# A planner's model of transfers gets figures of its own for the start of the program, and nineteen ranks of a fused attention and MoE kernel are moved

## The chip, the cores and the metric

The kernel runs on one core of a Trainium2 chip. The engines are PE (matrix products; PEld is its loading of weights), DVE and ACT (elementwise work), POOL and SP (here they issue transfers). The metric is the device time of one execution in microseconds, lower is better.

## The reference

Eight batches of eight heads, 512 local and 32 global tokens a batch, head size 64. A local query sees the 32 global keys and the local keys within 32 places; a global query sees all 544 keys. The outputs of all heads of a token, put side by side (512 wide), go through a layer with a hard swish.

```python
s_g = scale * np.matmul(q_g, k_all.transpose(0, 1, 3, 2))
out_g = np.matmul(sm(s_g), v_all)
s_ll = scale * np.matmul(q_l, k_l.transpose(0, 1, 3, 2))
mask = np.abs(pos[:, None] - pos[None, :]) <= window
s_ll = np.where(mask, s_ll, -1000000000.0)
s_lg = scale * np.matmul(q_l, k_g.transpose(0, 1, 3, 2))
a_l = sm(np.concatenate([s_lg, s_ll], axis=-1))
out_l = np.matmul(a_l, np.concatenate([v_g, v_l], axis=2))
...
h = x @ w_in                       # (4352, 512) @ (512, 2048)
g = h * np.clip(h + 3.0, 0.0, 6.0) / 6.0
out = g @ w_out                    # (4352, 2048) @ (2048, 512)
```

## The kernel before

**Planned, not looped.** The body does not emit instructions in the order of its loops. `add` records an operation with its engine (or a choice of two), its planned duration, what it depends on, the buffer rings it takes and frees, and a `key`, its rank. `Plan.lay` then plays these operations on a model of the engines: at each moment it starts, on each engine, the operation that can start soonest, and among those that can start within 40 ns of it the one with the lowest key. A copy that ACT or DVE may do goes to the one that would finish it first. The order found in this way is emitted, and each engine runs its own queue in that order. So a key or a planned time does nothing to the chip but through the order of the queues, the choice of ACT or DVE, and `Plan.fill`, which puts idle matmuls ("filler", line 1017) on PE where the plan sees it wait before the first use of the second A bank: a filler step is planned at 440 ns (twice that before 5 us) and their number is the planned gap divided by that.

**Transfers.** The model of transfers (`Transfers`) has two queues, POOL's loads and SP's, which share the DMA engines. A transfer of so many packets of so many ns each begins `FIRST` after its issue and takes packets x ns / 16, slower when both queues are busy (`BESIDE`, `EVEN`). A queue has eight lanes: a transfer is issued when the eighth before it has landed. A row load has 12.4 ns a packet, a w_in or w_out load 85, a strip 86 or 300.

**The stages of a batch b.** `load_qk` (line 410) brings q and k of 128 tokens (one j of four), `load_v` V in five pieces (i of five), `load_g` the global q and k of two batches. The transfers from POOL are issued in the order of their keys alone. `turn_qk` and `turn_g` transpose by PE, through PSUM ring T (one buffer) or M (three), and a copy; from batch 4 or 5 on SP transposes by DMA. `strips_moved` lays V out as overlapping strips `st`, by seven transfers that SP issues once V is in (batch 0: some by copies, `strips_kept`). `place_kg` puts the global keys in place. `local_step` (b, j) is one attention step of 128 queries: scores on PE into the one S buffer (lines 655 to 669), eight masked reductions on DVE (681), eight exponentials on ACT (692), normalising on DVE (702, 706), eight transposes on PE (713), a copy, products with the strips on PE into the banks A0 and A1 (735, 743; two half steps from batch 1 on), and copies into `xt`. `global_steps` does the global queries (781 to 856); it takes S, A0 and A1. `moe_local` then makes the first product of a batch, w_in times `xt` (`first`, line 870), its hard swish on ACT (877) and DVE (881), and the second, with w_out (`second`, line 894), and SP stores the result (908).

**Ranks.** Steps of batch b get keys near 4b, and loads lie earlier by `AHEAD`. For batch 0 the list `seq` ranks the loads one by one (from -8.0 in steps of 0.05: q0 to q3, v0 to v4, w_in, then the global loads); w_out follows from -6.0 on, among batch 1's loads (from -6.6 in steps of 0.1).

```python
self.queue[o.eng].append([o.start + self.FIRST[o.eng] + wait, packets * ns / 16, o])
...
s, o = min(((s, o) for s, o in starts if s <= s0 + 40), key=lambda x: (x[1].key, x[1].n))
...
n = round(gap / one) if at < self.EARLY else int((gap - 100) / one)
```

Of the kernel before, what the change touches and what calls it, by code (L numbers as in the profile page):

```python
# [75 lines left out]


class Plan:  # L80
# [4 lines left out]
    COLD, FILL, EARLY = 5000.0, 440.0, 12000.0  # L85
# [123 lines left out]
def kernel(  # L209
# [20 lines left out]
    NJ = Sl // P  # L230
# [712 lines left out]

    xgd = {}
    lqk, lg, keyT, kg0_op = {}, {}, {}, []
    for b in range(B):
        if b == 0:
            seq, APART = ["q0", "h", "q1", "q2", "v0", "v1", "v2", "q3", "v3", "v4", "i0", "i1", "i2", "i3", "g"], (0.11, 0.001)  # L950
            for n, what in enumerate(seq):
                k, i, key = what[0], int(what[1:] or 0), -8.0 + 0.05 * n
                if k == "q":
                    lqk[0, i] = load_qk_direct(0, i, key) if i < 2 else load_qk(0, i, key, 1, APART[i - 2])
                elif k == "h":
                    halo = load_halo(key)
                elif k == "g":
                    lg[0] = []
                    for n, (i, k) in enumerate(((0, 0), (0, 1), (1, 0), (1, 1))):
                        lg[0].append(load_g(0, i, k, key + 0.001 * n, lg[0][0] if n else None))  # L960
                elif k == "v":
                    vload[0, i] = load_v(0, i, key)
                else:
                    wi[i] = load_w_in(i, key)
            for c in range(0, NDFF, 4):
                wo[c] = wo[c + 1] = wo[c + 2] = wo[c + 3] = load_w_out(c // 4, W_OUT + 0.05 * c)
        else:
            base = -6.6 if b == 1 else 4.0 * b - 3.0 - AHEAD
            stepk = 0.1 if b == 1 else 0.4
            for j in range(NJ):  # L970
                lqk[b, j] = load_qk(b, j, base + j * stepk)
            if b % 2 == 0:
                lg[b // 2] = []
                for i in range(2):
                    for k in range(2):
                        lg[b // 2].append(load_g(b, i, k, base + (1.5 + 0.1 * i + 0.05 * k) * stepk,
                                                 lg[b // 2][0] if lg[b // 2] else None))
            for i in range(NV):
                vload[b, i] = load_v(b, i, base + (i + 3.5) * stepk)
        if b == 0:  # L980
            for js in BLOCKS:
                s_ = (strips_kept if js[0] < KEEP else strips_moved)(b, list(js), 4.0 * b - 3.5 + 0.9 * js[0])
                for j in js:
                    strip[b, j] = s_
        else:
            for j in range(NJ):
                strip[b, j] = strip[b, j - 1] if j else strips_moved(b, list(range(NJ)), base + 1)
        strip[b] = {j: strip[b, j] for j in range(NJ)}
        lead = 4.0 * b - 4.0 if b < 2 else 4.0 * b - AHEAD
        if b % 2 == 0:  # L990
            if b == 0:
                head = turn_direct(0, lqk[0, 0], halo)
                kg[0] = head.pop()
                gT[0] = turn_g(0, lg[0], lead + 0.5, [kg[0]])
                if KEEP < NJ:
                    kg0_op.append(place_kg(0, lead - 1.2 if KEEP == 0 else lead + 0.9, kg[0]))
            else:
                gT[b // 2] = turn_g(b, lg[b // 2], lead - 1.5)
        if b:
            kg[b] = place_kg(b, lead - 1.2)  # L1000
        for j in range(NJ):
            if b == 0 and j < 2:
                o = turn_direct(j, lqk[0, j]) if j else head
                qkT[0, j], keyT[0, j] = o[0], o[1:]
            elif b == 0:
                keyT[b, j] = [turn_qk(b, j, lqk[b, j][:1], lead + j - 1.5, (1,))]
                qkT[b, j] = turn_qk(b, j, lqk[b, j], lead + j - 1.5, (0,))
            else:
                qkT[b, j] = turn_qk(b, j, lqk[b, j], lead + j - 1.5)
# [3 lines left out]
        xgd[b] = global_steps(b, lead + 3.6)  # L1013
        moe_local(b, 4.0 * b + 0.5, 4.0)
    moe_global(4.0 * b + 2.5, 1.5)

    order = plan.fill(plan.lay(), lambda: nc.tensor.matmul(  # L1017
        out=psA[1][:, 0:256], lhsT=idle.bitcast(FP32)[:, 0:P], rhs=idle.bitcast(FP32)), "A1")
# [36 lines left out]
```

## Time and profile before

| what | us |
|---|---|
| median of 3 runs (lowest to highest) | 333.57 (333.43 to 334.77) |
| the profiled execution's own time | 332.85 |
| its span, first to last instruction | 331.1 |
| PE busy | 317.9 (96%) |
| DVE busy | 265.3 (80%) |
| ACT busy | 254.0 (77%) |
| POOL busy | 106.1 (32%) |
| transfers of the POOL queue, share of 16 engines' span | 71.3% |
| transfers of the SP queue, the same | 46.5% |

How to read it: times are microseconds from the first instruction. A line of the profile names source line, engine, operation and the tiles it writes and reads; `x8` is a count. "idle before" and `<-` tell how long an engine stood idle before an instruction and what released it. PE's busy time counts a matmul from its start to a modelled end, so waits can hide in it; starts are exact. A row of the stage table gives a stretch, its length, then busy time and instruction count of PE, PEld, DVE, ACT and POOL, the granted PE clock as a share of full speed, the DMA share and GB/s.

### The profile page before, as it was taken

The numbers are of one execution on the slowest core, as the hardware profiler recorded it, in microseconds if no ns is written. First come the engines' busy times: TensorE is split into PE (matmuls) and PEld (weight loads), VectorE is DVE, ScalarE is ACT, GpSimd is POOL, SyncE is SP. The second block draws the span as 40 slices with busy tenths as digits, with TensorE's granted clock in tenths as the row PEclk, the third lists the DMA queues.
The fourth block names the chain that finished last, engine by engine and source line by source line (L and its number), as shares of the span: only waits on it lengthen the run. The fifth ranks groups of instructions, "written<-read, shape, count | busy, mean of one in ns | idle before, by whom it ended". The sixth has DMA issues, their size and how long they took to land.

```text
span 331.1 us, 10240 instructions
## 1 busy us (share of the span) xinstructions
PE 317.9 (96%) x3824; PEld 184.9 (56%) x3824; DVE 265.3 (80%) x997; ACT 254.0 (77%) x851; POOL 106.1 (32%) x139
## 2 busy tenths in 40 slices
PE   8999968989999999999999999999999999999996
PEld 6778855456556554555554545454445544546644
DVE  4899799779998799898998799689988896385400
ACT  4899798579989499887995789699988994464402
POOL 8725942497292845613460050004000000000000
PEclk9999999999999999999999999999999999999999
DMA  9999999999999999999999999999984214400013
GB/s 160 184 251 172 128 196 264 161 200 223 218 174 206 203 157 174 214 225 168 129 176 250 242 122 194 197 193 178 205 135 120 63 36 110 91 0 2 32 56 104
DMA packets 158738, 52.25 MB, mean 158 GB/s; under 512 B 142944, under 2 KB 151392, under 8 KB 158688
## 3 DMA queue, kind: packets, MB, share of 16 engines
q0 software_dynamic: 106560, 17.05, 71.3%
q1 hardware_dynamic: 52128, 34.55, 46.5%
q8 instruction: 30, 0.49, 0.6%
q14 instruction: 20, 0.16, 0.2%
HBM read 35.26 MB, written 8.91 MB: 133 GB/s over the span
## 4 chain that ended last, share of the span: by engine, by line
PE 64%; DVE 15%; ACT 9%; issue 2%; ACTq 0%; DVEq 0%
PE m L894 31%; PE m L870 24%; DVE gs L881 4%; ACT sm L692 3%; DVE sm L681 3%; PE a L743 3%; ACT t L877 2%; DVE pn L706 2%; PE s L669 2%; DVE pg L821 2%; ACT sg L807 2%; PE t L713 1%; PE s L662 1%; ACT xt L296 1%; DVE et L298 1%
## 5 line engine op out<-in xcount | busy, mean ns | idle before, releaser
L894 PE MATMUL m<-wout,gs 128*128 128x512 f16 (+1 forms) x560 | 129.7, 373 | 0.0
L870 PE MATMUL m<-xt,win 128*128 128x512 f16 (+1 forms) x576 | 122.1, 355 | 1.8 <-DVE gs L881 0.9
L692 ACT ACTIVATE sm<-sm,stat 128x128 f32<-128x128 f32 x256 | 100.9, 398 | 11.1 <-DVE stat L681 10.5
L881 DVE SCALAR_TENSOR_TENSOR gs<-t,m 128x512 f16<-128x512 f32 x136 | 91.6, 683 | 17.2 <-ACT t L877 15.9
L877 ACT ACTIVATE t<-m 128x512 f32<-128x512 f32 x136 | 80.7, 599 | 22.2 <-PE m L870 21.1
L870 PEld LDWEIGHTS <-win 128*128 128x128 f16 x640 | 59.3, 98 | 52.5 <-issue 3.3
L894 PEld LDWEIGHTS <-gs 128*128 128x128 f16 x560 | 51.1, 98 | 49.9 <-issue 1.4
L681 DVE CUSTOM_DVE_ANT_0 sm<-s,mask 128x128 f32<-128x128 f32 x256 | 61.7, 282 | 2.2 <-PE s L669 1.1
L692 ACT ACTIVATION_READ_ACCUMULATOR sm<-sm,stat 128x1 f32 x256 | 50.0, 195 | 0.0
L706 DVE TENSOR_TENSOR pn<-sm,stat 128x512 f16<-128x512 f32 x64 | 44.0, 687 | 0.6
L296 ACT CAST xt<-a 64x256 f16<-64x256 f32 (+1 forms) x83 | 31.0, 374 | 7.5 <-PE a L743 6.6
L411 POOL DMA_DIRECT2D ve<-in_v_l_dram x40 | 32.2, 822 | 10.6 <-PE t L592 6.5
L411 POOL DMA_DIRECT2D nat<-in_q_l_dram x30 | 27.0, 900 | 25.4 <-DMA qk<-nat 10.7
L411 POOL DMA_DIRECT2D nat<-in_k_l_dram x30 | 27.4, 915 | 15.6 <-DMA win<-in_moe_w_in_dram 5.2
L743 PEld LDWEIGHTS <-st 128*128 128x128 f16 x448 | 19.7, 98 | 11.3 <-issue 1.0
L296 ACT COPY ot<-m 128x512 f32<-128x512 f32 (+1 forms) x24 | 13.6, 571 | 13.2 <-PE m L894 12.7
L411 POOL DMA_DIRECT2D ve<-in_v_g_dram x8 | 4.8, 597 | 56.3 <-PE a L848 56.2
L743 PE MATMUL a<-et,st 128*128 128x64 f16 x448 | 22.1, 193 | 0.6 <-ACT xt L296 0.6
L681 DVE DVE_READ_ACCUMULATOR2_ANT stat<- 128x1 f32 x256 | 21.1, 82 | 0.0
L298 DVE CAST xt<-a 64x256 f16<-64x256 f32 (+1 forms) x33 | 14.1, 428 | 4.4 <-PE a L743 4.1
L702 DVE RECIPROCAL stat<-stat 128x4 f32<-128x4 f32 x64 | 11.1, 173 | 5.9 <-ACT sm L692 5.3
L1017 PE MATMUL a<-idle 128*128 128x256 f32 x46 | 14.6, 450 | 1.2 <-DVE idle L380 1.2
(88 smaller groups left out, 270.7 us busy)
## 6 DMA issues: line engine op xcount, KB each, us to landing
out_dram<-ot SPq DMA_DIRECT2D x31, 256.0 KB, 3.5
st<-ve SPq DMA_DIRECT2D x14, 384.0 KB, 7.4
nat<-in_k_l_dram POOLq DMA_DIRECT2D x30, 128.0 KB, 8.0
nat<-in_q_l_dram POOLq DMA_DIRECT2D x30, 128.0 KB, 8.4
st<-ve SPq DMA_DIRECT2D x7, 512.0 KB, 7.5
st<-ve SPq DMA_DIRECT2D x14, 256.0 KB, 7.7
ve<-in_v_l_dram POOLq DMA_DIRECT2D x24, 128.0 KB, 6.7
st<-ve SPq DMA_DIRECT2D x18, 128.0 KB, 7.3
```

The source lines that it names most:

```text
L296: nc.scalar.copy(out=out, in_=in_)
L298: nc.vector.tensor_copy(out=out, in_=in_)
L411: nc.gpsimd.dma_start(out=dst(op), in_=src)
L681: nc.vector.tensor_tensor_reduce(out=sm[sm_op.slot][:, h, :], in0=psS[s.slot][:, e, p * P:(p + 1) * P], in1=m, scale=-scale, scalar=3.0e38 ...
L692: nc.scalar.activation(out=sm[sm_op.slot][:, h, :], in_=sm[sm_op.slot][:, h, :], func=EXP, scale=-1.0, bias=stat[stat_op.slot][:, 0, h:h + 1],
L706: (nc.gpsimd if op.eng == "POOL" else nc.vector).tensor_tensor(out=pn[pn_op.slot][:, h0:h1, :], in0=sm[sm_op.slot][:, h0:h1, :], in1=stat[ ...
L743: nc.tensor.matmul(out=psA[a][:, c0:c0 + 64], lhsT=st[r][:, u * NJ + j, p * P:(p + 1) * P], rhs=et[et_op.slot][:, 2 * p:2 * p + 2, u * UQ: ...
L870: nc.tensor.matmul(out=psM[op.slot][:, i * n:(i + 1) * n], lhsT=w_in_t[:, m, (c + i) * P:(c + i + 1) * P], rhs=x()[:, m, t0:t0 + n], start ...
L877: nc.scalar.activation(out=t1[to.slot], in_=psM[f.slot], func=RELU, bias=0.5, scale=1.0 / 6.0)
L881: nc.vector.scalar_tensor_tensor(out=gs[set_.slot][:, c:c + k, t0:t0 + n], in0=t1[to.slot].rearrange("f (k t) -> f k t", k=k), scalar=1.0, ...
L894: nc.tensor.matmul(out=psM[(f or op).slot][:, 0:w], lhsT=gs[set_.slot][:, c, t0:t0 + P], rhs=w_out_t[:, c, cols], start=(c == 0), stop=(c ...
L1017: order = plan.fill(plan.lay(), lambda: nc.tensor.matmul(out=psA[1][:, 0:256], lhsT=idle.bitcast(FP32)[:, 0:P], rhs=idle.bitcast(FP32)), "A1")
```

## The change

`Transfers` gets other figures for what is issued early. Until 28 us (`EARLY`, which was 12 us and stood for something else) a row load counts 14.0 ns a packet in place of 12.4, a weight load 70.5 in place of 85, a short strip 75 in place of 86, and the two queues share by packet size alone. Until 13 us (`FULL`) a transfer begins later than `FIRST` says: from SP by 670 ns before 6 us and 3130 after, from POOL by 700 before 4 us and 470 after; before, SP's began 1000 later until 12 us.

`MOVED` adds an amount to nineteen ranks. A negative one makes the operation come earlier in its queues, as far as the plan lets it; an entry with two parts moves every load of its kind.

```diff
-    LANES, END, EARLY, LATE = 8, 300, 12000.0, 1000.0
+    LANES, END, EARLY, FULL = 8, 300, 28000.0, 13000.0
+    OF_EARLY = {12.4: 14.0, 85.0: 70.5, 86.0: 75.0}
...
-        wait = self.LATE if o.eng == "SP" and o.start < self.EARLY else 0
+        wait = 0
+        if o.start < self.EARLY:
+            ns = self.OF_EARLY.get(ns, ns)
+        if o.start < self.FULL:
+            wait = (670 if o.start < 6000 else 3130) if o.eng == "SP" else 700 if o.start < 4000 else 470
...
-            part = {h[2].eng: h[2].dma[1] + self.EVEN for h in heads}
+            even = 0 if self.now < self.EARLY else self.EVEN
+            part = {h[2].eng: h[2].dma[1] + even for h in heads}
...
+    MOVED = {("step", 0, 0): -1, ("step", 0, 3): -0.25, ("turn", 0, 2): 1, ("v", 0, 4): -1, ("w_in", 0): 0.5,
+             ("q", 1, 3): -0.5, ("step", 1, 1): 1, ("step", 1, 3): -2, ("v", 1, 2): 0.5, ("v", 1, 4): -1,
+             ("g", 2): -0.25, ("v", 2, 1): -0.5, ("v", 2, 3): -4, ("g", 4): 2, ("step", 4, 0): -0.5,
+             ("step", 5, 0): -0.5, ("step", 6, 2): 0.25, ("step", 6, 3): 0.25, ("step", 7, 3): 0.5}
...
+        def by(what, j=None):
+            return MOVED.get((what, b), 0.0) + MOVED.get((what, b, j), 0.0)
...
-            xdone[b, j] = local_step(b, j, lead + j)
+            xdone[b, j] = local_step(b, j, lead + j + by("step", j))
```

The other lines of the diff add `by(...)` in the same way to the keys of the loads (`q`, `g`, `v`, `w_in`, `w_out`), the strips, `turn_g`, the placing of keys, `turn_qk`, the global steps and the products; only the nineteen entries above are not zero. `Plan.EARLY`, a constant of `fill`, stays at 12 us.

In the queues as built, POOL's first load is now v(0,4); the four global loads of batches 0 and 1 stand ahead of the four of w_in; among the loads of batch 1, j = 3 of q and k and the last piece of V come before the others, and the piece v(1,2) stands behind three of the four w_out loads; v(2,3) comes right after the first q and k of batch 2. On PE the first scores of batch 0 come before the turn of its third q and k, the globals of batch 0 are turned right after the third scores (they were turned after nine groups of first products), batch 0's global step comes after four of its sixteen groups of first products (it came after eight), batch 1's steps run in the order 0, 1, 3, 2, and batch 0's second products all come before batch 1's products with the strips.

More of the change, by code (lines that the diff above doesn't have):

```diff
@@ L953 @@
                 if k == "q":
-                    lqk[0, i] = load_qk_direct(0, i, key) if i < 2 else load_qk(0, i, key, 1, APART[i - 2])
+                    lqk[0, i] = load_qk_direct(0, i, key) if i < 2 else load_qk(0, i, key + by("q", i), 1, APART[i - 2])
                 elif k == "h":
@@ L961 @@
                 elif k == "v":
-                    vload[0, i] = load_v(0, i, key)
+                    vload[0, i] = load_v(0, i, key + by("v", i))
                 else:
-                    wi[i] = load_w_in(i, key)
+                    wi[i] = load_w_in(i, key + by("w_in", i))
             for c in range(0, NDFF, 4):
-                wo[c] = wo[c + 1] = wo[c + 2] = wo[c + 3] = load_w_out(c // 4, W_OUT + 0.05 * c)
+                wo[c] = wo[c + 1] = wo[c + 2] = wo[c + 3] = load_w_out(c // 4, W_OUT + 0.05 * c + by("w_out", c // 4))
         else:
@@ L975 @@
                     for k in range(2):
-                        lg[b // 2].append(load_g(b, i, k, base + (1.5 + 0.1 * i + 0.05 * k) * stepk,
+                        lg[b // 2].append(load_g(b, i, k, base + (1.5 + 0.1 * i + 0.05 * k) * stepk + by("g"),
                                                  lg[b // 2][0] if lg[b // 2] else None))
             for i in range(NV):
-                vload[b, i] = load_v(b, i, base + (i + 3.5) * stepk)
+                vload[b, i] = load_v(b, i, base + (i + 3.5) * stepk + by("v", i))
         if b == 0:
             for js in BLOCKS:
-                s_ = (strips_kept if js[0] < KEEP else strips_moved)(b, list(js), 4.0 * b - 3.5 + 0.9 * js[0])
+                s_ = (strips_kept if js[0] < KEEP else strips_moved)(b, list(js), 4.0 * b - 3.5 + 0.9 * js[0] + by("strips", js[0]))
                 for j in js:
@@ L986 @@
             for j in range(NJ):
-                strip[b, j] = strip[b, j - 1] if j else strips_moved(b, list(range(NJ)), base + 1)
+                strip[b, j] = strip[b, j - 1] if j else strips_moved(b, list(range(NJ)), base + 1 + by("strips"))
         strip[b] = {j: strip[b, j] for j in range(NJ)}
@@ L997 @@
             else:
-                gT[b // 2] = turn_g(b, lg[b // 2], lead - 1.5)
+                gT[b // 2] = turn_g(b, lg[b // 2], lead - 1.5 + by("turn_g"))
         if b:
-            kg[b] = place_kg(b, lead - 1.2)
+            kg[b] = place_kg(b, lead - 1.2 + by("keys"))
         for j in range(NJ):
@@ L1005 @@
             elif b == 0:
-                keyT[b, j] = [turn_qk(b, j, lqk[b, j][:1], lead + j - 1.5, (1,))]
-                qkT[b, j] = turn_qk(b, j, lqk[b, j], lead + j - 1.5, (0,))
+                keyT[b, j] = [turn_qk(b, j, lqk[b, j][:1], lead + j - 1.5 + by("turn", j), (1,))]
+                qkT[b, j] = turn_qk(b, j, lqk[b, j], lead + j - 1.5 + by("turn", j), (0,))
             else:
-                qkT[b, j] = turn_qk(b, j, lqk[b, j], lead + j - 1.5)
+                qkT[b, j] = turn_qk(b, j, lqk[b, j], lead + j - 1.5 + by("turn", j))
                 keyT[b, j] = [qkT[b, j]]
         for j in range(NJ):
-            xdone[b, j] = local_step(b, j, lead + j)
-        xgd[b] = global_steps(b, lead + 3.6)
-        moe_local(b, 4.0 * b + 0.5, 4.0)
-    moe_global(4.0 * b + 2.5, 1.5)
+            xdone[b, j] = local_step(b, j, lead + j + by("step", j))
+        xgd[b] = global_steps(b, lead + 3.6 + by("global"))
+        moe_local(b, 4.0 * b + 0.5 + by("products"), 4.0 + by("span"))
+    moe_global(4.0 * b + 2.5 + by("products_g"), 1.5)
     order = plan.fill(plan.lay(), lambda: nc.tensor.matmul(
```

4 lines of the change are left out of this document (2 added, 2 removed).

## The prediction

> **What bounds the kernel now.** I read the page first, then the busy time by stage.
>
> ```profile
> span 331.1 us, 10240 instructions
> ...
> 8.70:24.90 16.20, 14.93 (x373) 11.90 (x373) 14.57 (x75) 14.56 (x58) 8.12 (x12) 1.00 1.61 219
> 24.90:34.00 9.10, 8.93 (x128) 7.90 (x113) 8.22 (x29) 8.40 (x27) 5.23 (x6) 1.00 1.69 163
> 34.00:42.90 8.90, 8.43 (x166) 7.30 (x165) 7.21 (x17) 7.10 (x17) 8.90 (x13) 1.00 1.90 138
> 42.90:50.80 7.90, 4.60 (x99) 3.86 (x97) 7.82 (x43) 7.20 (x28) 3.56 (x5) 1.00 1.35 204
> 50.80:60.80 10.00, 10.00 (x140) 5.64 (x139) 9.81 (x46) 8.42 (x40) 1.28 (x3) 1.00 1.25 260
> 60.80:74.10 13.30, 11.42 (x142) 6.92 (x142) 9.51 (x23) 8.52 (x29) 11.32 (x15) 1.00 1.90 171
> ...
> 80.00:240.00 160.00, 158.43 (x1929) 85.30 (x1928) 145.95 (x558) 136.82 (x477) 55.86 (x70) 1.00 1.48 192
> 240.00:320.00 80.00, 80.00 (x684) 41.92 (x682) 52.53 (x155) 50.93 (x151) 0.00 (x0) 1.00 0.30 65
> ```
>
> Each stage row gives its length, then the busy time of PE, PEld, DVE, ACT and POOL, the clock, the DMA share. From 80 to 320 us PE is busy 238.43 of 240 us: 1.57 us in all can be won there. Up to 24.9 us PE's busy time is partly its idle-filling matmuls; DVE (14.57 of 16.20) and ACT (14.56) carry the softmax of batch 0. Between 24.9 and 74.1 PE idles 5.8 us (0.17, 0.47, 3.30, 0, 1.88). So a new order can win time before 74 us, and little after.
>
> PE in order of time, where it loses most:
>
> ```profile
> 42.93 0.44 PE L835 MATMUL t<-ident,pg 128*128 128x128 f16 x5
> 44.99 0.44 PE L835 MATMUL t<-ident,pg 128*128 128x128 f16 x5 [1.62 <-ACT eg L296]
> 45.37 0.35 PE L662 MATMUL s<-kgz,qk 128*128 128x32 f16 x8
> ...
> 48.29 0.39 PE L713 MATMUL t<-ident,pn 128*128 128x128 f16 x4
> ...
> 50.75 0.35 PE L662 MATMUL s<-kgz,qk 128*128 128x32 f16 x8 [0.87 <-DVE stat L681]
> ...
> 67.09 1.03 PE L894 MATMUL m<-wout,gs 128*128 128x512 f16 x4
> 68.58 0.39 PE L743 MATMUL a<-et,st 128*128 128x64 f16 x8 [0.46 <-ACT xt L296]
> 69.77 0.38 PE L612 MATMUL t<-ident,natg 128*128 128x128 f16 x4 [0.80 <-DVE et L298]
> ...
> 74.09 0.35 PE L662 MATMUL s<-kgz,qk 128*128 128x32 f16 x8
> ```
>
> From start to start, less about what the step itself takes: 42.93 to 44.99 loses 1.7 (five transposes take 0.38, 44.99 to 45.37), 48.29 to 50.75 loses 2.0, 67.09 to 68.58 loses 0.6, 68.58 to 69.77 loses 0.95. That is 5.25; with the smaller gaps I put it at 7. In the first two, PE stands behind a one-buffer ring (T, S).
>
> **The change, part by part.** The transfer figures emit no instruction; they shift planned starts, and with the 19 ranks they re-sort the queues. The built orders hold the same steps (438 on PE, 134 on POOL, 143 on SP), one filler step less on PE, and 60 copies that change between ACT and DVE. The first 82 PE steps, up to batch 2's first scores (74.09 above), are one set in both. So the sum is: when PE comes to that step, and what is lost behind it.
>
> *The first 28 us.*
>
> ```profile
> 3.48 2.34 PE L1017 MATMUL a<-idle 128*128 128x256 f32 x5
> 5.62 1.24 PE L459 MATMUL m<-ident,sm 128*128 128x128 f32 x8
> ...
> 7.22 0.46 PE L459 MATMUL m<-ident,t 64*128 64x64 f32 x4
> ...
> 8.70 0.24 PE L655 MATMUL s<-qk 64*32 64x96 f16 x8
> ...
> 24.90 1.92 PE L870 MATMUL m<-xt,win 128*128 128x256 f16 x16
> ...
> 13.26 0.74 POOL L411 DMA_DIRECT2D win<-in_moe_w_in_dram  x1
> ...
> win<-in_moe_w_in_dram POOLq DMA_DIRECT2D x1, 512.0 KB, 17.0
> ...
> 17.70 0.58 POOL L411 DMA_DIRECT2D natg<-in_k_g_dram  x1
> ...
> natg<-in_k_g_dram POOLq DMA_DIRECT2D x1, 32.0 KB, 13.4
> ...
> sm<-in_k_l_dram SPq DMA_DIRECT2D x1, 256.0 KB, 6.2
> ...
> 24.10 0.56 ACT L296 CAST xt<-a 128x512 f16<-128x512 f32 x1
> ...
> 35.49 0.39 DVE L628 COPY kgz<-gt 64x128 f16<-64x128 f16 x2
> 36.02 0.69 DVE L298 COPY qk<-t 128x1024 f16<-128x1024 f16 x1
> 36.63 1.22 DVE L794 TENSOR_REDUCE stat<-s 128x2 f32<-128x1024 f32 x1
> ...
> 38.34 0.68 DVE L881 SCALAR_TENSOR_TENSOR gs<-t,m 128x512 f16<-128x512 f32 x1
> ```
>
> Four filler steps stand at the start, not five: the first turn comes at 4.8, not 5.62 (a filler step is two matmuls of 0.43 to 0.47, from the first row). Two fillers now stand before the halo turn: 6.8, not 7.22. The turn of keys 2 (turn(0,2) +1, step(0,0) -1) no longer stands before the first scores: about 8.05, not 8.70. That 0.65 isn't kept. The second k load (issued near 3.9, in 6.2 later, at 10.1) holds the next step. The key copy of batch 1, 0.5 on DVE (35.49 to 36.02), now comes ahead of step (0,3), whose rank by -0.25 changes a place. Copies that come to DVE early and those that leave it balance. DVE reaches the first gate of a product at 28.1, as now; bounds 0.6 either way.
>
> The q_g and k_g loads now go ahead of w_in (+0.5), v(0,4) goes to POOL's front. By the place in the queue natg is in at about 18, not 31.1 (17.70 + 13.4); w_in comes 0.6 later: 30.9 instead of 30.3 (13.26 + 17.0), and PE wants it near 35, so 0 (if 4 us later than that, 1 for 1). The turn of batch 0's globals goes from 34 to about 20, and 0.35 of PE leaves the stretch. Its copy comes on ACT before step 2's exponentials, and step 1's xt copy (24.10) now comes after them: the first product starts at 25.65, 0.75 later than 24.90.
>
> *The global step of batch 0* is ready 5 us sooner; its reduction, 1.7 on DVE (36.63 to 38.34), stands ahead of product evictions. With three M buffers the sixth product group waits for those: it comes at 34.1, with 1.65 lost, and a copy through T after it costs 0.75. Bounds of both: 1.0 (one eviction of 0.68 overtakes) to 3.1.
>
> *Transfers at 37 to 66 us.*
>
> ```profile
> L411 POOL DMA_DIRECT2D wout<-in_moe_w_out_dram x4: 794/808/813, 38.0 to 41.7; - x4
> ...
> DMA to landing us min/median/max: 8.3/11.7/20.1
> ...
> SPq L536 <- DMA ve<-in_v_l_dram: 9.7, 1, 9.7
> ...
> 49.34 4.29 SPq L536 DMA_DIRECT2D st<-ve  x6
> ...
> st<-ve SPq DMA_DIRECT2D x1, 256.0 KB, 8.5
> ```
>
> The w_out loads land 8.3 to 20.1 after issue, the last at 61.8, since the last two share the engines with batch 1's strips, which SP issues from 49.34 to 53.6, after 9.7 of waiting for V, and which are in at 61.5 (the last issued at 53.0, plus 8.5): 12.2 from first issue to last landing. v(1,2) by +0.5 puts a V piece behind three w_out loads; v(1,4) by -1 and q(1,3) by -0.5 pull theirs ahead. My estimate from these rows: w_out in by 50, 52.6 and 56.5, the V piece at 53.3, the strips at 53.3 + 12.2 = 65.5. Batch 0's second products are free some 5 us sooner, and step(1,1) by +1 and step(1,3) by -2 spread batch 1's scores between them. The places of 42.93 and 48.29 then have products behind them: both losses go (at worst half of them stays, 1.8). v(2,3) by -4 makes POOL wait for batch 0's global output near 44; behind it stand only batch 2's loads, used 15 us later: 0. v(2,1) by -0.5 and g(2) by -0.25 move inside that queue: 0.
>
> ```profile
> L296 ACT CAST xt<-a 64x256 f16<-64x256 f32 (+1 forms) x83 | 31.0, 374 | 7.5 <-PE a L743 6.6
> L298 DVE CAST xt<-a 64x256 f16<-64x256 f32 (+1 forms) x33 | 14.1, 428 | 4.4 <-PE a L743 4.1
> ```
>
> What is late next: batch 1's outputs now follow all of batch 0's second products, and PE reaches them at 67.7. Eight half steps (0.23 each, 2.5 with the turns between) go through two A banks. A bank takes a half step and two copies of 0.374 or 0.428 and the hand-overs, 1.35; four times, 5.4, of which 2.9 is lost.
>
> *Sum to 74 us.* 74.09 + 0.75 (start) - 0.35 (turn moved out) - 7.0 + (1.65 + 0.75 + 2.9 + 0.4 of small gaps = 5.7) = 73.2: 0.9 won.
>
> *Behind it.* g(4) by +2 (natg still lands some 10 us before use), step(4,0) and (5,0) by -0.5, (6,2) and (6,3) by +0.25, (7,3) by +0.5: scores and softmax, and from batch 5 their SP transposes, move past products and stores (7 SP entries by two places or more). Of the 1.57 I take 0.6 as won; bounds 1.57 won, 1.5 lost (as much again as now).
>
> The profiled execution is 332.85 (span 331.1 and 1.75 around it), 0.72 under the median of 333.57. Less 1.5: 331.35, and 332.05 as the median.
>
> **The rivals.**
> - *Both halves come out well*: the M wait is 1.0 in all instead of 2.4, the banks turn in 1.2, the late idle goes: 0.9 + 1.4 + 0.6 = 2.9, and 1.0 behind: some 3.5 won, 330.1 to 331.2. For it: the M wait hangs on one DVE row of 1.7. Against: DVE is 90% busy there.
> - *The loss is only moved*: M wait 3.1 (0.7 more), a bank turn of 1.5 (0.6 more), as much late idle as now: 0.9 - 1.3 = 0.4 lost, 334.0. For it: ACT 8.40 and DVE 8.22 of 9.10 leave no room. That nothing moves at all is excluded: 171 PE steps change by two places or more.
> - *Slower: batch 1's strips come late.* All eight half steps wait for them; up to 67.7 that is free, beyond it each us is one of the end. Were the V piece in only at 57 and the strips slowed by batch 2's loads to 14.5, they land at 71.5: 3.8 - 1.5 = 2.3 lost, 335.9. For it: the last two w_out loads beside strips took 10 us. Against: this V piece travels before the strips start.
> - *The clock.* Every row grants 1.00, also 42.90:50.80 where PE idles 3.3 of 7.9. Were it halved at 67.7, the 2.5 of PE work there would cost up to 2.5 more: 1.0 lost, 334.6. The Trainium skill ("TensorE: Matmul & The Clock Gate", Part 1: The HAM clock gate) has the clock fall to half after an idle window of some 3.4 us, and fewer fillers go against that rule; the rows at 42.93 and 48.29 show gaps of 2 us without it. Chance 0.02, within the moved loss.
>
> **How the numbers follow.** Forecast (331.2 to 332.8) 0.45, of which 0.20 lies under 331.9; good case 0.19; moved loss (332.8 to 335.2) 0.25; slower 0.11. 0.5%, about what a measurement of this kernel tells from no change, is 1.67 us: under 331.9 is 0.39, over 335.2 is 0.11, between them 0.50. The range 330.2 to 334.9 leaves out the slower case and the ends of two others, some 0.2; the likeliest case's own is 331.2 to 332.8.
>
> **What would show it.** Right: first scores near 8.05, globals turned near 20, first product near 25.6, 1 to 2 us lost near 33, no gap over 1 us from 36 to 66, strips in before 67, batch 2's first scores near 73.2, under 1.6 idle on PE from 80 us. Wrong: PE waiting for strips or w_out, batch 2's first scores after 74.5, or more idle behind 80 us than now.

## The result, and the profile after

On the chip of the first comparison the changed kernel takes 330.58 us (median of 22 runs, 328.89 to 335.61), the kernel before 334.38 (22 runs): ratio 0.9897, 95% interval 0.9869 to 0.9924. On another chip (the run `e11_changed_again` below) it is 330.97 against 333.32, ratio 0.9936, 0.9902 to 0.9970. So the change wins 2 to 3.5 us; the two intervals together leave 1.0 to 4.4. The ratios leave out executions more than 1.5% above the fastest of their kernel. The forecast was 332.05, a ratio of 0.9954 to the median it started from: the right direction, but less than came. 330.58 lies inside the whole range that was given (330.2 to 334.9) and below the likeliest one (331.2 to 332.8).

The profiled execution took 329.59 us, its span is 327.8 (before: 332.85 and 331.1). First its busy time by stage, cut at what the trace shows; the columns are those of the table of before (length, then busy time of PE, PEld, DVE, ACT and POOL, the clock, the DMA share, GB/s):

```profile
24.00:34.00 10.00, 8.02 (x151) 6.65 (x151) 9.61 (x35) 8.52 (x29) 4.75 (x6) 1.00 1.76 188
34.00:43.00 9.00, 8.30 (x150) 7.52 (x148) 7.34 (x21) 6.81 (x16) 7.50 (x10) 1.00 1.92 181
43.00:51.00 8.00, 8.00 (x128) 6.45 (x126) 7.92 (x32) 7.77 (x26) 2.64 (x5) 1.00 1.34 218
51.00:61.00 10.00, 10.00 (x148) 5.29 (x147) 9.10 (x52) 9.61 (x46) 4.08 (x5) 1.00 1.65 229
61.00:73.00 12.00, 10.39 (x166) 7.02 (x164) 8.82 (x29) 9.44 (x30) 10.03 (x13) 1.00 2.01 206
...
80.00:240.00 160.00, 158.68 (x1909) 85.26 (x1908) 146.95 (x551) 136.41 (x479) 53.36 (x67) 1.00 1.51 190
240.00:320.00 80.00, 80.00 (x684) 42.08 (x682) 50.11 (x148) 49.28 (x143) 0.00 (x0) 1.00 0.28 62
```

From 43 to 61 us PE doesn't idle at all; before, the 7.9 us from 42.9 held 3.3 us of idle. What PE loses now lies at 24 to 34 (1.98, of which a part is ahead of the first product) and at 61 to 73 (1.61). PE in order of time shows the places (start, busy time, and in brackets how long PE stood idle before and what released it):

```profile
19.73 0.39 PE L618 MATMUL t<-ident,natg 128*128 128x128 f16 x4
...
24.91 1.03 PE L876 MATMUL m<-xt,win 128*128 128x256 f16 x8 [0.35 <-ACT xt L302]
...
33.34 2.78 PE L876 MATMUL m<-xt,win 128*128 128x256 f16 x24 [1.63 <-DVE gs L887]
...
37.88 0.61 PE L598 MATMUL t<-ident,nat 128*128 128x128 f16 x8 [0.70 <-ACT qk L302]
...
66.27 0.63 PE L749 MATMUL a<-et,st 128*128 128x64 f16 x16
67.50 0.74 PE L749 MATMUL a<-et,st 128*128 128x64 f16 x16 [0.60 <-ACT xt L302]
...
71.26 0.35 PE L668 MATMUL s<-kgz,qk 128*128 128x32 f16 x8
```

Line numbers are six higher than before. 19.73 is the turn of batch 0's globals (34 before), 33.34 the sixth product group behind the M ring, 37.88 the wait for the copy through T, 66.27 the first product of batch 1 with its strips, 71.26 batch 2's first scores, which stood at 74.09: 2.83 won by then. Behind them the span still runs 256.5 us (257.0 before), so 0.5 is won there.

### The profile page after: what moved, and what is told of

Read it like the earlier page. It is cut to its first block, busy times and chain, and to the rows that moved or that the text cites. A ratio compares the mean times of both kernels' runs of the same rounds, so it can differ in the third digit from the quotient of the medians.

```text
span 327.8 us, 10243 instructions
## 1 busy us (share of the span) xinstructions
PE 316.1 (96%) x3822; PEld 184.5 (56%) x3822; DVE 266.0 (81%) x997; ACT 254.5 (78%) x851; POOL 105.7 (32%) x139
## 4 chain that ended last, share of the span: by engine, by line
PE 79%; DVE 10%; ACT 6%; DMA 3%; issue 1%; SPq 1%; ACTq 0%
PE m L900 35%; PE m L876 30%; PE a L749 4%; DVE sm L687 3%; ACT sm L698 3%; PE s L675 2%; DVE pn L712 2%; PE t L719 2%; DMA et<-pn 2%; DVE gs L887 2%; PE s L668 2%; ACT t L883 1%; ACT xt L302 1%; PE t L598 1%; DMA t<-in_k_g_dram 1%
## 5 line engine op out<-in xcount | busy, mean ns | idle before, releaser
L687 DVE CUSTOM_DVE_ANT_0 sm<-s,mask 128x128 f32<-128x128 f32 x256 | 60.7, 283 | 3.4 <-PE s L675 2.7
L698 ACT ACTIVATION_READ_ACCUMULATOR sm<-sm,stat 128x1 f32 x256 | 49.3, 193 | 0.0
L304 DVE CAST xt<-a 64x256 f16<-64x256 f32 (+1 forms) x34 | 14.8, 435 | 5.2 <-PE a L749 4.9
L1029 PE MATMUL a<-idle 128*128 128x256 f32 x44 | 13.5, 440 | 1.2 <-DVE idle L386 1.2
L719 PE MATMUL t<-ident,pn 128*128 128x128 f16 x160 | 12.6, 219 | 0.4 <-DVE pn L712 0.2
## 6 DMA issues: line engine op xcount, KB each, us to landing
out_dram<-ot SPq DMA_DIRECT2D x31, 256.0 KB, 3.4
st<-ve SPq DMA_DIRECT2D x14, 256.0 KB, 8.8
```

The lines of the kernel that those rows point to most:

```text
L304: nc.vector.tensor_copy(out=out, in_=in_)
L687: nc.vector.tensor_tensor_reduce(out=sm[sm_op.slot][:, h, :], in0=psS[s.slot][:, e, p * P:(p + 1) * P], in1=m, scale=-scale, scalar=3.0e38 ...
L698: nc.scalar.activation(out=sm[sm_op.slot][:, h, :], in_=sm[sm_op.slot][:, h, :], func=EXP, scale=-1.0, bias=stat[stat_op.slot][:, 0, h:h + 1],
L719: nc.tensor.matmul(out=psT[op.slot][:, h * P:(h + 1) * P], lhsT=pn[pn_op.slot][:, h, :], rhs=ident, is_transpose=True)
```

## The experiments

For each kernel I read three distances off its profile: when the first product comes, the way from there to batch 2's first scores ("middle"), and from there to the end of the span ("rest"); beside them PE's waits for the transposed softmax weights (`et<-pn`) behind 80 us, from the view of waits. Ratios are to the kernel before, on the same chip.

| kernel | first product | middle | rest | waits for `et` | clock dropped | ratio (95%) |
|---|---|---|---|---|---|---|
| before | 24.90 | 49.19 | 257.0 | none shown | 49 of 98 | 1 |
| changed | 24.91 | 46.35 | 256.5 | 0.5 | 6 of 22 | 0.9897 (0.9869 to 0.9924) |
| changed again (e11) | 25.61 | 46.35 | 258.8 | 3.3 | 2 of 12 | 0.9936 (0.9902 to 0.9970) |
| e1 figures only | 24.73 | 47.55 | 261.6 | 1.4 | 2 of 6 | 1.0102 (1.0048 to 1.0155) |
| e2 first thirteen ranks | 24.94 | 46.35 | 257.6 | 0.8 | 0 of 12 | 0.9948 (0.9921 to 0.9976) |
| e3 V piece first | 24.36 | 51.43 (d) | 258.2 | 2.0 | 6 of 12 | 0.9959 (0.9923 to 0.9996) |
| e4 reduction later | 25.15 | 48.49 (d) | 255.6 | none shown | 11 of 12 | 0.9930 (0.9897 to 0.9963) |
| e5 late six ranks | 24.94 | 50.14 (d) | 258.1 | 0.2 | 5 of 12 | 1.0024 (0.9984 to 1.0064) |
| e6 ranks, old figures | 26.16 | 50.73 (d) | 262.8 (d) | 4.5 | 6 of 6 | 1.0192 (1.0142 to 1.0243) |
| e7 one more filler | 25.64 | 46.34 | 257.4 | 1.9 | 0 of 12 | 0.9931 (0.9903 to 0.9960) |
| e8 batch 1 in order | 25.13 | 48.31 | 259.2 (d) | 2.0 | 5 of 12 | 1.0002 (0.9966 to 1.0038) |
| e9 one filler less | 25.37 | 46.34 | 256.0 | 0.7 | 4 of 12 | 0.9917 (0.9883 to 0.9950) |
| e10 gate both ways | 25.39 | 46.69 | 259.8 (d) | 2.4 | 5 of 12 | 0.9955 (0.9916 to 0.9993) |

"Clock dropped" counts the executions whose mean granted clock is 0.995 or less, and (d) marks the distance in which it happened in the profiled one. Such a drop lasts about 3.4 us at half the clock, worth up to 1.7 us; its rows stand with the clock below. Means of 0.998 and 0.999 are not counted: the profiled execution of e1 has 0.998, and its clock falls only at the very end, when PE has no work left.

The five executions whose middle has the changed kernel's order and no drop (changed twice, e2, e7, e9) agree on it within 0.01 us, while their first product wanders by 0.7 and their rest by 2.8. (e12, below, has 46.33.) So the middle can be read from one profile in which the clock doesn't drop there. In the rest the waits for `et` come and go. Less these waits, and 1.7 for a drop, it is 255.3 to 256.2 in all eight executions that have both the new figures and all of the nineteen ranks behind 74 us (changed twice, e3, e4, e7 to e10); 257.0 before, 256.8 in e2, 257.9 in e5, 260.2 in e1.

**e1: the figures alone.** `MOVED` is emptied.

```diff
-    MOVED = {("step", 0, 0): -1, ...}
+    MOVED = {}
```

> The new transfer figures stay, none of the nineteen ranks is moved. Theory (the time is won before 74 us by the ranks: w_out ahead of the V piece, batch 1's steps spread): the gaps of 1.7 to 2 us on PE near 43 and 48 us are there again, batch 2's first scores come at 73.5 to 74.5, and the time is 0.996 to 1.003 of before. Rival (the figures alone re-sort the early queues well): batch 2's first scores at 71 to 72 and 0.989 to 0.992 of before.

PE in order of time, and the stage row of 80 to 240 us:

```profile
44.10 0.44 PE L841 MATMUL t<-ident,pg 128*128 128x128 f16 x5 [1.04 <-ACT eg L302]
...
49.86 0.35 PE L668 MATMUL s<-kgz,qk 128*128 128x32 f16 x8 [0.86 <-DVE stat L687]
```

```profile
80.00:240.00 160.00, 155.50 (x1875) 83.46 (x1873) 144.32 (x541) 133.34 (x464) 54.63 (x69) 1.00 1.54 191
```

The wait near 48 is back as the theory had it, the one near 43 in part (1.04 us, before 1.62). But the middle, 47.55, is 1.64 us shorter than before: the figures alone bring more than half of the 2.84 that the change wins there, and batch 2's first scores come at 72.28, between what the theory and the rival said. Beside the shorter wait near 43, PE idles 0.7 us in the ten from 60.7 us, where the kernel before idles 1.7 in the ten from 60.9. And yet the whole isn't as fast as before but slower: 1.0102. The loss lies where neither theory looked: from 80 to 240 us PE idles 4.5 us in place of 1.57. New figures for the first 28 us re-lay the whole queue behind them, and what they laid there is worse.

**e6: the ranks alone.** The transfer figures are those of before, the nineteen ranks stay. (One dependence of the planner is added, that the scores of a step of batch 1 wait for the turn of the keys before it.)

```diff
-    LANES, END, EARLY, FULL = 8, 300, 28000.0, 13000.0
-    OF_EARLY = {12.4: 14.0, 85.0: 70.5, 86.0: 75.0}
+    LANES, END, EARLY, LATE = 8, 300, 12000.0, 1000.0
```

> The nineteen ranks with the transfer figures of before (and one stated dependency on the previous keys for batch 1's scores, which changes no queue of the changed kernel). Theory (ranks carry the gain, the figures only place fillers and ties): batch 2's first scores by 72.3, 0.989 to 0.994 of before. Rival (the ranks fit only the new figures' order): 0.996 to 1.004.

```profile
38.69 0.61 PE L592 MATMUL t<-ident,nat 128*128 128x128 f16 x8 [1.25 <-DMA ve<-in_v_l_dram]
40.54 1.01 PE L592 MATMUL t<-ident,nat 128*128 128x128 f16 x8 [0.63 <-ACT qk L296]
...
53.76 0.35 PE L662 MATMUL s<-kgz,qk 128*128 128x32 f16 x8 [1.39 <-DVE stat L681]
...
229.33 0.39 PE L743 MATMUL a<-et,st 128*128 128x64 f16 x8 [1.61 <-DMA et<-pn]
237.04 0.39 PE L743 MATMUL a<-et,st 128*128 128x64 f16 x8 [2.18 <-DMA et<-pn]
```

1.0192, slower than theory and rival had it: the same ranks in another laid order put PE behind other transfers and copies. All six executions have a clock drop, the profiled one two, so a part of the 1.9% is clock. Neither half of the change gains time by itself; what the ranks are worth hangs on the order that the figures lay.

**e2 and e5: the ranks divided.** e2 keeps the new figures and the thirteen ranks up to `("v", 2, 3)`, e5 the new figures and the six from `("g", 4)` on.

```diff
-             ("g", 2): -0.25, ("v", 2, 1): -0.5, ("v", 2, 3): -4, ("g", 4): 2, ("step", 4, 0): -0.5,
-             ("step", 5, 0): -0.5, ("step", 6, 2): 0.25, ("step", 6, 3): 0.25, ("step", 7, 3): 0.5}
+             ("g", 2): -0.25, ("v", 2, 1): -0.5, ("v", 2, 3): -4}
```

> The new figures and the thirteen ranks of batches 0 to 2; the six later ones (g of batch 4, steps of batches 4 to 7) are not moved. The queues up to some 85 us are those of the changed kernel. Theory (nearly all is won before 74 us): batch 2's first scores at 71.3, PE idle from 80 us 1.5 to 2.0, and 0.990 to 0.993 of before. Rival (the six late ranks carry a part of their own of 1.5 us or more): 0.994 to 0.997, with idle from 80 us over 2.5.

> The new figures and the six late ranks alone (g of batch 4, steps of batches 4 to 7). Theory (nearly all is won before 74 us by the early ranks): batch 2's first scores at 73.5 to 74.5 as in the kernel before, 0.994 to 1.000 of before. Rival (the late ranks carry most): 0.989 to 0.992.

e2 has the whole gain of the middle (46.35). e5 has the two waits near 43 and 48 again, and a clock drop behind the second; its middle is 50.14, or 48.4 less 1.7 for the drop:

```profile
44.86 0.44 PE L841 MATMUL t<-ident,pg 128*128 128x128 f16 x5 [1.60 <-ACT eg L302]
...
50.62 0.35 PE L668 MATMUL s<-kgz,qk 128*128 128x32 f16 x8 [0.86 <-DVE stat L687]
```

So the two waits go with the thirteen ranks. These bring 1.2 us of the middle's gain over e1 and 2.1 over e5; what is left of the 2.84 (1.64 and 0.8) comes with the figures. The six are worth 0.6 to 1.5 us by the rest without its waits (256.8 in e2, 255.3 to 256.2 with them), and 2.3 from e1 to e5 (260.2 to 257.9). These are single profiles, though. e2's ratio, 0.9948, lies where its rival had it, but the intervals don't separate it from the changed kernel (0.9897 and 0.9936).

**e3: the V piece ahead of w_out again.** In POOL's queue the piece v(1,2) goes back ahead of the w_out loads.

```diff
     order = plan.fill(plan.lay(), ...)
+    # the load of v(1,2), which stands behind three of w_out, goes ahead of the first
+    put(325, before=32)
```

> The changed kernel with one load moved on POOL alone: the V piece v(1,2) goes ahead of the four w_out loads again, as before the change; every other queue stays as it is in the changed kernel. Theory (the late V piece is what lets w_out land without the strips beside it): strips issued near 45.5 instead of 50.7, the last two w_out loads land at 54 to 58 instead of 49.9 and 53.3, PE waits for them with its second products at 53.0 and 56.7, and the run is 1 to 4 us slower than the changed kernel (0.993 to 1.002 of before). Rival (the order of these loads is hidden anyway): within 0.5 us of the changed kernel, 0.988 to 0.992.

```profile
53.23 2.75 PE L900 MATMUL m<-wout,gs 128*128 128x512 f16 x12 [0.66 <-DMA wout<-in_moe_w_out_dram]
59.67 2.72 PE L900 MATMUL m<-wout,gs 128*128 128x512 f16 x6 [2.64 <-DMA wout<-in_moe_w_out_dram]
...
70.80 0.63 PE L749 MATMUL a<-et,st 128*128 128x64 f16 x16
```

In brackets is the changed kernel. The piece lands at 40.7 (50.7), so SP issues the strips from 47.28 on (50.72), and the last w_out comes in beside them at 59.6 (53.3). Not all of these 6.3 us come from the strips: the first w_out lands 2.4 us later too, at 44.4, before any strip of batch 1 is issued, since the piece now goes ahead of it. PE waits 3.3 us for w_out, the gap of 2.64 is followed by 3.1 us at half the clock (some 1.6 more), and the middle is 5.1 longer. The place behind w_out keeps the piece and the strips out of w_out's way. The ratio, 0.9959, loses 0.2 to 0.6% of 330 us to the changed kernel's two: 1 to 2 us, within what the intervals leave open. In half of e3's executions the clock doesn't drop, and how late w_out lands in those was not profiled.

**e4 and e10: the wait of the sixth product group.** At 33.34 PE waits 1.63 us, since on DVE the reduction of batch 0's global scores stands ahead of the product evictions. e4 puts that reduction, and its exponentials on ACT, behind three more evictions. e10 moves by hand what hangs on it as well: the exponentials behind the swish of two groups and the key turn's copy, the reciprocal behind two more evictions, and two first products ahead of the transposes of `pg`.

```diff
+    put(204, after=241)   # reduction, DVE: behind the evictions of c4, c6, c8
+    put(206, after=244)   # its exponentials, ACT
+    put(208, after=248)
```

> The changed kernel with three instructions of batch 0's global step put later in their queues: its reduction on DVE behind three product evictions that stand after it, its two pairs of exponentials on ACT each behind one relu. Theory (the 1.6 us on PE before the sixth product group is that reduction standing ahead of the evictions, and the global chain has some 1.3 us to spare): that gap is under 0.4, first products end 1.0 to 1.6 earlier, batch 2's first scores at 69.9 to 70.6, 1 to 1.6 us faster than the changed kernel, 0.985 to 0.988 of before. Rival (the wait only moves: to the transposes of the global weights near 40 us, or to batch 1's strips, in at 64.1): the gap goes, another of the same size comes before 71 us, and the time is within 0.4 us of the changed kernel.

> Edit: the stretch from 31 to 45 us laid out anew by hand. The reduction of batch 0's global scores goes behind three product evictions, and what follows it goes later as well: its exponentials behind the swish of groups c10, c12 and the key turn's copy, its reciprocal behind the evictions of c12 and c14; two more first products stand ahead of the transposes of pg. Theory (the 1.63 us wait of the sixth product group can be taken out if everything behind the reduction on DVE and ACT moves with it): c10 at 31.8, turn (1,1) near 36.4 (37.88), no wait over 0.6 from 31 to 45, batch 2's first scores near 69.8 (71.26), 1.4 us shorter in all, ratio to the kernel before near 0.986. Rival (DVE is the bound in this stretch, 9.61 busy of 10.00 from 24 to 34, so the wait comes back at other places): waits of 1 to 2 us in sum between 36 and 52, batch 2's first scores near 71.3 or later, ratio 0.990 or more.

e4, PE in order of time:

```profile
31.83 2.78 PE L876 MATMUL m<-xt,win 128*128 128x256 f16 x24
...
38.64 0.61 PE L598 MATMUL t<-ident,nat 128*128 128x128 f16 x8 [2.81 <-ACT qk L302]
```

e10, by stage:

```profile
24.00:34.00 10.00, 9.25 (x162) 7.90 (x163) 9.66 (x35) 8.20 (x28) 3.88 (x5) 1.00 1.75 191
34.00:43.00 9.00, 8.28 (x146) 7.09 (x145) 6.92 (x23) 7.48 (x19) 8.38 (x11) 1.00 1.90 163
43.00:51.00 8.00, 6.80 (x117) 5.33 (x115) 7.67 (x25) 7.01 (x22) 2.25 (x4) 1.00 1.33 220
```

Both take the wait away, and by their profiles both pay it back; their ratios (0.9930 and 0.9955) don't differ from the changed kernel's by more than the intervals. In e4 PE waits 2.81 for a copy on ACT that now stands behind the exponentials, the clock drops after it (11 of 12 executions), and the middle grows by 2.1. In e10 that wait is 0.49, but from 43 to 51 us, where the changed kernel's PE idles nothing, 1.20 is lost, and the middle is 0.3 longer than without the edit. Between 24 and 34 us DVE is busy 9.6 of 10: the wait looks like DVE's work rather than the order of it. My theory fell in both. e10's rival was right; e4's had the wait come back at the same size, and it came back larger.

**e8: batch 1's steps in order.** The two ranks of the attention steps of batch 1 are dropped, so they run 0, 1, 2, 3.

```diff
-             ("q", 1, 3): -0.5, ("step", 1, 1): 1, ("step", 1, 3): -2, ("v", 1, 2): 0.5, ("v", 1, 4): -1,
+             ("q", 1, 3): -0.5, ("v", 1, 2): 0.5, ("v", 1, 4): -1,
```

> The changed kernel without its two entries for batch 1's steps (step 1 by +1, step 3 by -2). Theory (the spread of batch 1's scores takes away the gap at 48 us): a gap of 1 to 2 us on PE between 47 and 51 us, batch 2's first scores up to 1 us later than 71.3, 0.3 to 1.2 us slower than the changed kernel. Rival (w_out in time is enough, the scores find products beside them in any order): no gap over 0.5 us there, and within 0.3 us of the changed kernel.

```profile
50.18 0.35 PE L668 MATMUL s<-kgz,qk 128*128 128x32 f16 x8 [1.27 <-DVE stat L687]
```

The wait for the S buffer near 48 is back, and the middle is 2.0 longer, 1.27 of it by this wait. At a ratio of 1.0002 no gain is left. e7, below, has the changed kernel's middle and ran on the same chip at 0.9931; to it e8 loses 0.7%, some 2.4 us, and the middle's 2.0 are most of that. The drop and the wait of 2.0 near 225 in this profile are among those that come and go. The order 0, 1, 3, 2 is what puts products behind the place where PE waited for S; the wait near 43 stays away without it.

**e7, e9 and e11: the start.** e7 puts one more filler step at the very start, e9 takes out one of the two between the halo turn and the first scores, e11 is the changed kernel once more, on the chip and beside the runs of e9 and e10.

```diff
+    order.insert(order.index(one), Op("PE", 880.0, one.emit, ...))   # e7
...
+    order.remove(idles[4])                                           # e9
```

> The changed kernel with one more filler step (two idle matmuls, 0.85 us) at the start of PE's queue, so five as before; no other queue changes. Theory (the 0.85 us that the first scores are earlier are lost again before the first product, by the k load at 9.7 us and the extra key copy on DVE): first scores at 8.5 to 8.7, first product at 24.9 to 25.2, the time within 0.3 us of the changed kernel. Rival (the early start carries through): first product at 25.5 or later and 0.6 to 0.9 us slower.

> Edit: of the two filler steps that stand between the halo turn and batch 0's first scores one is taken out (two idle matmuls of 0.53). Theory (a shift of the start is kept): in the changed kernel those fillers run from 6.80 to 7.86 while the last key copy ends near 7.4; the first scores come at about 7.4, and the first product and batch 2's first scores move by as much: 24.5 and 70.8; the whole is 0.4 us shorter, which the medians can hardly show (ratio to the kernel before 0.987 to 0.990). Rival (the start is not kept, since DVE's and ACT's queues of batch 0's softmax or a transfer set the pace): first scores at 7.4, first product still near 24.9.

> The changed kernel once more, beside the two others on the same chip, so that differences of some tenths are read against it. Theory: a ratio to the kernel before of 0.987 to 0.992, first scores at 7.5 to 7.9 (as the key halo lands), batch 2's first scores 63.4 us behind the first scores, as in the first profile (71.26 less 7.86). Rival (the stages shift against each other from one execution to the next): that distance differs by over 0.5.

PE in order of time, e7, then e9, then e11:

```profile
7.02 0.43 PE L465 MATMUL m<-ident,t 64*128 64x64 f32 x4 [0.87 <-DMA t<-in_k_g_dram]
...
8.44 0.24 PE L661 MATMUL s<-qk 64*32 64x96 f16 x8
```

```profile
7.33 0.24 PE L661 MATMUL s<-qk 64*32 64x96 f16 x6
...
25.37 1.03 PE L876 MATMUL m<-xt,win 128*128 128x256 f16 x8 [0.35 <-ACT xt L302]
```

```profile
6.89 0.43 PE L465 MATMUL m<-ident,t 64*128 64x64 f32 x4 [0.70 <-DMA t<-in_k_g_dram]
...
8.31 0.24 PE L661 MATMUL s<-qk 64*32 64x96 f16 x8
...
25.61 1.03 PE L876 MATMUL m<-xt,win 128*128 128x256 f16 x8 [0.35 <-ACT xt L302]
...
194.91 0.39 PE L749 MATMUL a<-et,st 128*128 128x64 f16 x8 [1.39 <-DMA et<-pn]
...
225.36 0.44 PE L749 MATMUL a<-et,st 128*128 128x64 f16 x8 [1.88 <-DMA et<-pn]
```

Alone, e7 looks like proof that a later start is kept: first scores 0.58 later than in the changed kernel, first product 0.73 later. e11 takes that back. The same kernel, with no filler added, starts as late by itself (8.31 and 25.61), and in both PE waits for the halo of keys and not for fillers. e9 is the test from the other side: first scores 0.53 earlier than in the first profile, first product 0.46 later. There the earlier start isn't kept: at 18.79 PE waits 1.13 us for a strip of batch 0 that landed at 18.65 (17.67 in the first profile). The first product comes between 24.4 and 25.6 in the kernels with the changed kernel's order up to it, as the first transfers happen to land. From the first scores to batch 2's it is 63.65 us in e11 (63.4 was expected) and 64.38 in e9. Neither e7 nor e9 differs in time from the changed kernel by more than the intervals.

**e12: V behind the transpose.** The V loads of batches 6 and 7 wait until the transpose of softmax weights beside them has landed.

```diff
+    for turn, loads in ((1470, range(1655, 1661)), (1698, range(1909, 1915))):
+        # POOL copies four elements of that transpose's result, and then issues the loads
+        order[here:here] = [Op("POOL", 100.0, look(by_n[turn]), ...), *loads]
```

> Edit: the V loads of batches 6 and 7, which POOL issues as soon as their buffer is free (183.7 and 217.7 in the changed kernel), wait until the transpose of softmax weights that SP issues at the same moment has landed (a copy of four elements on POOL, ahead of the loads, reads its result). Theory (the waits of 0.5 to 2.4 us that PE has near 194 and 225 us in some executions, each released by that transpose, come from the V loads beside it): the two transposes land 3 to 3.5 us after issue in place of 7.3 to 8.8 and 5.4 to 6.2, near 189 and 220; no wait over 0.5 on PE near 194 and 225; the V loads begin 5 and 2.5 us later and the strips of batches 6 and 7 land by 208 and 239, ahead of their first products (209.5 and 241.4). The stretch from batch 2's first scores to the end is that of the first profile of the changed kernel, not that of the second (2.3 us longer); ratio to the kernel before 0.984 to 0.989. Rival 1 (the strips then come late): PE waits at 209 or 241 for 1 to 3 us, ratio 0.990 or more. Rival 2 (the transpose is slow by itself or through stores and other turns): it still lands 5 us or more after issue, the waits stay.

By a mistake of this edit, batch 7's loads also went ahead of a global product on PE that still needs the old V in that buffer; it then waits for the new V, 10.8 us, and computes with it. So the whole time (ratio 1.0352, 1.0319 to 1.0386) says nothing of the theory, and I read the two transposes and the stretch up to 215 us alone. Issues of the transpose, with us to landing, in the changed kernel, then in e11, then in e12, at 186 and at 216 to 222 us:

```profile
et<-pn SPq DMA_TRANSPOSE x1, 7.3
...
et<-pn SPq DMA_TRANSPOSE x1, 5.4
```

```profile
et<-pn SPq DMA_TRANSPOSE x1, 8.8
...
et<-pn SPq DMA_TRANSPOSE x1, 6.2
```

```profile
et<-pn SPq DMA_TRANSPOSE x1, 3.9
...
et<-pn SPq DMA_TRANSPOSE x1, 3.1
```

Without the V loads beside them the transposes take 3.9 and 3.1 us, and PE has no wait near 194. Rival 2 is out: these two transposes were slow because of the V loads beside them. The first is the better evidence, since at the second PE already stands idle. But the loss moves on, much as rival 1 had it: SP issues the strips of batch 6 later, the last of them lands at 210.2 (203.7 in the first profile), the next transpose is issued only behind them, at 207.0 (200.2), and PE waits for that:

```profile
211.16 0.41 PE L749 MATMUL a<-et,st 128*128 128x64 f16 x8 [1.07 <-DMA et<-pn]
```

Whether a V load that waits less would gain was not tried. No version here measurably beats the changed kernel.

## Why the prediction came out as it did

Up to batch 2's first scores the mechanism was the forecast one, step by step; what was off there were sizes, all on the cautious side. The time fell where the rival "both halves come out well" stood (chance 0.19), not in the likeliest range (0.45). Two things weren't in the account: the clock, and that the figures without the ranks already win 1.64 us of the middle (e1).

- *First scores near 8.05, globals turned near 20*: right, 7.86 and 19.73.
- *The losses at 43 and 48 go*: right. No idle from 43 to 61 us. e5 shows that the thirteen ranks do it, e8 that for the second it is the order of batch 1's steps, and e3 that the order of V piece, w_out and strips must go with them. w_out landed at 42.0, 47.3, 49.9 and 53.3 (forecast: all in by 56.5), the piece at 50.7 (53.3), the strips at 64.1 (65.5).
- *The sixth product group*: right to the tenth. From the first product to it were forecast 8.45 us, with 1.65 lost; measured 8.43 (24.91 to 33.34), with 1.63, and 0.70 for the copy through T where 0.75 stood. The rival that hoped for 1.0 in all there got 2.33, and e4 and e10 didn't get it lower without paying elsewhere.
- *From there to batch 1's products with the strips*: forecast 33.6, measured 32.9. I put PE's losses of before at 7.0 in all and new small gaps at 0.4; the sum of small gaps was too coarse by 0.7.
- *The bank turn*: 5.4 and 2.9 lost were forecast for the eight half steps, 66.27 to 71.26 is 5.0 with the turns between. The loss was too large and the work too small: PE idles 1.6 of the 5.0 (0.60, 0.31 and 0.38 for ACT's copies, 0.33 for one of DVE's) and works 3.4, where the forecast had 2.9 and 2.5.
- *The start*: "the first product starts at 25.65, 0.75 later" was a term of the sum, and it isn't one. The first profile has 24.91, the second 25.61. It is spread of the first loads, which I took from one execution as a fixed delay. By what it does to the sum this is the largest mis-sized term: without it my own sum gives 331.3 as the median. "That 0.65 isn't kept" holds (e9).
- *Behind batch 2's first scores*: 0.6 won was forecast; 0.5 was won in the first profile, and 1.8 lost in the second, by waits for `et<-pn` of 3.3. Without these waits it is 1.0 to 1.5 (257.0 to 256.0 and 255.5). I had counted the late idle as a matter of order alone; part of it is one transfer beside others, which changes from one execution to the next.
- *Together*: middle 2.84 won (49.19 to 46.35), where the same forecast steps give 1.64 (25.65 to 73.2 is 47.55). The rival "both halves come out well" has the time (330.1 to 331.2) but not the reason: the M wait and the late idle that it counted on hardly shrank. Nor is its sum right: 0.9 + 1.4 + 0.6 and 1.0 behind are 3.9, not 3.5, which is 329.7.
- *The slow rivals*: the strips weren't late. "That nothing moves" was excluded rightly. What I lacked was a rival in which figures and ranks are worthless apart: e1 and e6 are both slower than before.
- *The clock*: I gave it 0.02, from rows of one execution, which showed gaps of 2 us without a drop. That step fell. Below are stage rows of the kernel before and of e5, the same two gaps near 49 us and then the 3.4 us from half a microsecond behind them, and the same of e4's gap:

```profile
48.67:50.75 2.08, 0.40 (x6) 0.28 (x5) 2.08 (x16) 2.08 (x8) 1.29 (x2) 1.00 1.23 209
...
51.20:54.60 3.40, 3.40 (x52) 1.93 (x30) 3.40 (x12) 3.06 (x15) 0.58 (x1) 1.00 1.19 261
```

```profile
48.55:50.62 2.07, 0.40 (x5) 0.28 (x6) 2.07 (x16) 2.07 (x8) 1.48 (x3) 1.00 1.26 208
...
51.10:54.50 3.40, 3.40 (x44) 1.82 (x17) 2.88 (x10) 2.81 (x13) 0.58 (x1) 0.51 1.20 253
```

```profile
35.84:38.64 2.80, 0.00 (x0) 0.02 (x1) 1.37 (x4) 2.80 (x8) 2.80 (x5) 1.00 2.29 161
...
39.50:42.80 3.30, 3.30 (x22) 2.50 (x20) 2.03 (x4) 0.92 (x2) 2.40 (x3) 0.50 1.53 192
```

In these two the drop comes after PE is back at work, some 0.5 to 0.9 us later, in e3 just before it; whether it comes differs between executions with the same gap. It came in 49 of 98 executions of the kernel before, whose PE idles 1.62 us near 44 and 0.81 and 0.87 near 49 with 0.4 of work between; in 8 of 34 of the changed kernel, which has one such wait, 1.63 near 33, and none near 49; in 11 of 12 of e4 with its 2.8. So the change seems to win twice: where no clock dropped (on the chip of e11, 332.6 us before and 330.8 changed), and by fewer drops. That the fewer drops come from the gaps that went is argued, since only the profiled executions show where a drop was, and drops follow the long waits for `et` too (e8, e10: near 226); e2, e7 and e9, with the changed kernel's middle, have 0, 0 and 4 of 12. Over all runs the median of the kernel before is 332.6 us without a drop and 334.6 with one, of the changed kernel 330.1 and 333.2. The Trainium skill ("TensorE: Matmul & The Clock Gate", Part 1: The HAM clock gate) has the clock halve after an idle window of some 3.4 us that runs freely. The 3.4 us of a drop and its dependence on chance agree with such a window; that it takes 3.4 us of idle doesn't: here 2.07 us with PE busy 0.40 of them were enough.

## What to carry to other kernels

A planner's model and its ranks are one thing: changing the figures re-lays everything behind them, so judge both together, and look for the loss far behind the edit. Read one profile only for what repeats: here a stretch held to 0.01 us from one execution to the next, while the start and the waits on late transfers moved by 0.7 and 2.8 us, and a gap of 2 us on PE cost up to 1.7 more in clock in some executions and nothing in others. A wait that stood behind a full engine (DVE, 9.6 of 10) came back a few steps later here when it was taken away by order alone.

## What was not expected of the hardware

A transpose by DMA of softmax weights took 3.1 and 3.9 us from issue to landing without V loads beside it (e12; in the changed kernel the four from 234 us on, after the last V load, 3.0 to 3.9), and 5.4 to 8.8 beside the five or six V loads that POOL issued in the same microseconds, even where it was issued first (216.95, the first V load at 217.72, landed at 222.30). The Trainium skill ("DMA: Bandwidth & Descriptors", Queues, rings and completion order) says that each engine takes turns between its queues packet by packet; the direction agrees, the packets themselves are not shown here. How long it takes differs between executions of one kernel (7.3 and 8.8; 5.4 and 6.2), and PE's waits behind it, 0.5 us in one and 3.3 in the other, are most of what the two profiled executions of the changed kernel differ by (327.8 and 330.8). The other thing, the clock that halves for 3.4 us behind gaps of 2 us, stands above.
